# Prologue of a Fourier filter and MLP-mixer kernel: six inputs in flight, TensorE sums of first token weights and filter products, one table, a filter part on GpSimd's queue

## Chip, cores, metric

One core of one Trainium2 chip. The metric is device time in microseconds; each version was run several times on the chip that also ran the kernel before, and only runs of the same (fast) state are compared. "Faster" and "slower" need 2%. Single places in a trace are given as microseconds from the start of the span.

## The reference

```python
def _attn_ref(x, filt_r, filt_i):              # x (8, 3008, 256), filters (1505, 256)
    X = np.fft.rfft(x, axis=1)
    Y = X * (filt_r + 1j * filt_i)[None, :, :]
    return np.fft.irfft(Y, n=x.shape[1], axis=1).astype(np.float32)

def _moe_ref(x, w_tok1, w_tok2, w_ch1, w_ch2): # (3008,256) (256,3008) (256,1536) (1536,256)
    xt = x.transpose(0, 2, 1)
    h = np.maximum(xt @ w_tok1, 0.0) @ w_tok2
    u = x + h.transpose(0, 2, 1)
    return (u + np.maximum(u @ w_ch1, 0.0) @ w_ch2).astype(np.float32)
```

The weights come as float64; the kernel reads their words and rounds them to float32 itself ("conversion").

## The kernel before

The transform of length 3008 = 64 x 47 is done in two matmul stages. Here stage A is the length-64 transform of batch 0 (12 units, result z written to memory), stage B the 32 length-47 steps with the filter (`b_unit`: matmul and multiplication, `bi_unit`: inverse matmul), stage C the conversion of the second token weights and two channel-weight tiles; then the mixer starts, beside which the other batches are filtered. The parts that matter:

```python
    def rounded(st, n, parts, late=False):        # conversion of one weight tile
        ...
        nc.scalar.activation(out=top, in_=hi_f, func=AF.Copy, scale=2.0 ** -112)
        nc.vector.tensor_scalar(out=top_i, ...)            # four VectorE operations
        ...
        for src, dst in parts:                             # and the sum of the two halves
            nc.vector.tensor_tensor(out=dst, in0=src(top), in1=src(rest), op=ALU.add)

    def w1_fold(i):                               # first token weights times a DFT table
        ps = bank("po%d" % (i % 2))
        w = w1[:, 2 * i:2 * i + 2, :].rearrange("p a t -> p (a t)")
        nc.tensor.matmul(ps, wai_t, w, start=True, stop=True)
        nc.scalar.copy(out=w, in_=ps)

    def wc1_load(i, late=True):                   # channel weights: load, later convert, combine
        st = stage(512)                           # waits for a free stage buffer
        for g in range(CB):
            nc.gpsimd.dma_start(...)
        yield
        rounded(...)
        if c == DH - 1:
            combine(wc1[:, 2 * q:2 * q + 2])      # five GpSimd operations

    def weights():
        ...
        n = len(steps)                            # 12 + 16 + 2 tiles before the mixer
        steps += [f(i) for f, i in LAST]          # ten channel-weight tiles in the mixer
        ...
        load(AHEAD)                               # AHEAD = 6
        yield
        for i, s in enumerate(steps):
            next(s, None)                         # converts tile i
            load(not n - 2 <= i < n)              # loads one tile ahead, save in two places
            yield

    def b_unit(k):
        ps = bank(("b", "pg")[k % 2] if first else "b")...
        nc.tensor.matmul(ps, wbs[k // WC][:, k % WC, :], t2s[k // KC][:, k % KC], ...)
        ...
        nc.vector.tensor_tensor(out=p1, in0=ps, in1=fr, op=ALU.mult)
        nc.vector.scalar_tensor_tensor(out=p2[re], in0=ps[im], scalar=-1.0, in1=fi, ...)
        nc.vector.tensor_tensor(out=p2[im], in0=ps[re], in1=fi, op=ALU.mult)
        nc.vector.tensor_tensor(out=p1, in0=p1, in1=p2, op=ALU.add)
        prods[k] = p1
```

## Time and profile before

| | kernel before |
|---|---|
| time, median of 4 runs | 2663.66 us (2662.44 to 2665.65) |
| span and mean granted TensorE clock of the profiled run | 2662.7 us, 0.978 |
| first filter product (stage B begins) | 63.34 us |
| last filter product begins | 145.46 us |
| mixer's first matmul | 200.53 us |
| token sums of batch 1 | 552.23 us |
| last group of matmuls | 2643.01 us |

The last five are places of single instructions in the timeline. The granted clock is the share of full speed that the trace gives for TensorE. The stages by engine and the main waits are shown in the prediction.

### The profile page before, as it was taken

The numbers are of one execution on the slowest core, as the hardware profiler recorded it, in microseconds if no ns is written. First come the engines' busy times: TensorE is split into PE (matmuls) and PEld (weight loads), VectorE is DVE, ScalarE is ACT, GpSimd is POOL, SyncE is SP. The second block draws the span as 40 slices with busy tenths as digits, with TensorE's granted clock in tenths as the row PEclk, the third lists the DMA queues.
The fourth block names the chain that finished last, engine by engine and source line by source line (L and its number), as shares of the span: only waits on it lengthen the run. The fifth ranks groups of instructions, "written<-read, shape, count | busy, mean of one in ns | idle before, by whom it ended". The sixth has DMA issues, their size and how long they took to land.

```text
span 2662.7 us, 31542 instructions
## 1 busy us (share of the span) xinstructions
PE 2509.5 (94%) x10840; PEld 2000.5 (75%) x10840; DVE 1827.1 (69%) x3505; ACT 678.4 (25%) x1325; POOL 503.4 (19%) x926
## 2 busy tenths in 40 slices
PE   4667999999999999999999999999999999999997
PEld 1344766688787777788887777788888888888886
DVE  3886688846567788745658588755678586647675
ACT  2222322213222222212322122222222122212221
POOL 2324211111212111121211112121121121211221
PEclk8778999999999999999999999999999999999999
DMA  7664433222332222212233223211322111100000
GB/s 221 184 193 135 144 104 106 81 72 88 94 98 82 72 85 70 70 30 67 90 96 89 66 87 89 74 33 48 99 68 83 51 47 55 24 9 8 17 15 17
DMA packets 167158, 210.28 MB, mean 79 GB/s; under 512 B 35868, under 2 KB 115633, under 8 KB 166998
## 3 DMA queue, kind: packets, MB, share of 16 engines
q1 hardware_dynamic: 92937, 111.56, 13.9%
q0 software_dynamic: 30976, 44.53, 6.8%
q10 hardware_dynamic: 43085, 52.17, 6.0%
q8 instruction: 86, 1.41, 0.2%
q14 instruction: 74, 0.61, 0.1%
HBM read 133.15 MB, written 74.97 MB: 78 GB/s over the span
## 4 chain that ended last, share of the span: by engine, by line
PE 73%; DVE 18%; DMA 3%; issue 3%; ACT 2%; POOL 0%; SPq 0%; ACTq 0%; DVEq 0%; POOLq 0%
PE ps_po L526 25%; PE ps_pg L492 15%; PE ps_pg L508 11%; PE ps_acc L452 6%; PE ps_acc L435 5%; DVE t L470 3%; PE ps_acc L457 3%; DVE hh L470 3%; PE ps_b L382 3%; PE ps_b L349 3%; PE ps_acc L398 2%; DVE u L470 2%; DVE s L470 2%; DMA x<-in_x_dram 1%; DVE p L392 1%
## 5 line engine op out<-in xcount | busy, mean ns | idle before, releaser
L470 DVE TENSOR_TENSOR hh<-ps_pg,s 128x512 f32<-128x512 f32 (+3 forms) x864 | 482.7, 586 | 638.1 <-ACT s L495 637.5
L571 POOL DMA_DIRECT2D out_dram<-r x757 | 409.7, 550 | 1964.3 <-ACT hh L513 889.1
L513 ACT ACTIVATE hh<-hh 128x512 f32<-128x512 f32 (+1 forms) x576 | 347.9, 621 | 1110.6 <-DVE hh L470 1110.6
L526 PE MATMUL ps_po<-t,wc 128*128 128x256 f32 (+1 forms) x2304 | 536.1, 376 | 4.1 <-DVE t L470 3.0
L526 PEld LDWEIGHTS ps_po<-t,wc 128*128 128x128 f32 x2304 | 435.3, 190 | 127.8 <-issue 49.8
L492 PE MATMUL ps_pg<-v,wc 128*128 128x256 f32 (+1 forms) x1728 | 419.5, 380 | 2.5 <-POOL wc L275 2.4
L526 PE MATMUL ps_po<-hh,wc 128*128 128x256 f32 (+1 forms) x1728 | 413.5, 376 | 3.1 <-ACT hh L513 3.1
L492 PEld LDWEIGHTS ps_pg<-v,wc 128*128 128x128 f32 x1728 | 331.8, 193 | 43.3 <-POOL wc L275 2.8
L526 PEld LDWEIGHTS ps_po<-hh,wc 128*128 128x128 f32 x1728 | 328.5, 191 | 42.1 <-ACT hh L513 5.1
L508 PE MATMUL ps_pg<-u,wc 128*128 128x256 f32 (+1 forms) x1152 | 294.3, 378 | 9.1 <-DVE hh L470 9.0
L470 DVE TENSOR_TENSOR t<-t,hh 128x256 f32<-128x256 f32 (+1 forms) x576 | 243.5, 423 | 19.8
L508 PEld LDWEIGHTS ps_pg<-u,wc 128*128 128x128 f32 x1152 | 215.7, 190 | 48.6 <-DVE hh L470 23.6
L470 DVE TENSOR_TENSOR s<-ps_pg,hh 128x512 f32<-128x512 f32 (+1 forms) x288 | 196.1, 681 | 31.4 <-DVE hh L470 1.8
L452 PE MATMUL ps_acc<-w,h 128*128 128x512 f32 (+1 forms) x384 | 180.0, 591 | 15.8 <-ACT h L441 11.6
L470 DVE TENSOR_TENSOR t<-hh 128x512 f32<-128x512 f32 (+1 forms) x288 | 193.2, 671 | 0.6 <-ACT hh L513 0.6
L435 PE MATMUL ps_acc<-t,w 128*128 128x256 f32 x768 | 169.6, 383 | 6.2 <-DMA t<-g_tmp 5.0
L492 PE MATMUL ps_pg<-u,wc 128*128 128x256 f32 (+1 forms) x576 | 171.9, 381 | 0.4 <-DVE hh L470 0.4
L398 PE MATMUL ps_acc<-p,wi 128*96 128x512 f32 (+1 forms) x320 | 145.4, 537 | 26.5 <-DVE p L393 14.8
L508 PE MATMUL ps_pg<-v,wc 128*128 128x256 f32 (+1 forms) x576 | 168.9, 375 | 0.0
L435 PEld LDWEIGHTS ps_acc<-t,w 128*128 128x128 f32 x768 | 147.5, 193 | 27.7 <-issue 5.8
L382 PE MATMUL ps_b<-t,wb 96*128 96x512 f32 (+1 forms) x288 | 133.2, 545 | 21.9 <-DVE p L392 14.0
L495 ACT COPY s<-ps_pg 128x256 f32<-128x256 f32 (+1 forms) x288 | 105.8, 367 | 154.1 <-PE ps_pg L492 150.1
(67 smaller groups left out, 1949.5 us busy)
## 6 DMA issues: line engine op xcount, KB each, us to landing
z_tmp<-t ACTq DMA_DIRECT2D x96, 256.0 KB
t<-z_tmp SPq DMA_DIRECT2D x128, 192.0 KB
g_tmp<-t ACTq DMA_DIRECT2D x128, 192.0 KB
t<-g_tmp SPq DMA_DIRECT2D x48, 512.0 KB
x<-in_x_dram SPq DMA_DIRECT2D x184, 128.0 KB
out_dram<-r POOLq DMA_DIRECT2D x698, 32.0 KB, 1.8
wb<-wb_t SPq DMA_DIRECT2D x80, 96.0 KB
wi<-wi_t SPq DMA_DIRECT2D x80, 96.0 KB
```

The source lines that it names most:

```text
L349: nc.tensor.matmul(ps, wa, xs.pop((b, c)).rearrange("p a d -> p (a d)"), start=True, stop=True)
L382: nc.tensor.matmul(ps, wbs[k // WC][:, k % WC, :], t2s[k // KC][:, k % KC], start=True, stop=True)
L398: nc.tensor.matmul(ps[0:KR], wis[k // WC][:, k % WC, :], prods.pop(k), start=True, stop=True)
L435: nc.tensor.matmul(acc[:, t, :], w1[:, a, ts(t, P)], t4[b, a // TC4][:, a % TC4, :], start=(a == 0 and t == 0), stop=(a == A - 1 and t == ...
L452: nc.tensor.matmul(ps[:, 0:w], h1[:, t, ts(dh, P)], w2[:, t, ds(m * 512, w)], start=(t == 0), stop=False)
L470: nc.vector.tensor_tensor(out=out, in0=in0, in1=in1, op=op)
L492: nc.tensor.matmul(ps[:, 0:hw], wc1[:, jp, n, :], mov, start=True, stop=True)
L495: nc.scalar.copy(out=s[:, 0], in_=g[0][:, 0, 0:hw])
L508: nc.tensor.matmul(ps[:, 0:hw], wc1[:, jp, n, :], mov, start=True, stop=True)
L513: nc.scalar.activation(out=hs, in_=hs, func=AF.Relu)
L526: nc.tensor.matmul(po[i][:, j, 0:hw], wc2[:, jp, n, :], mov, start=(jp == 0 and first == 1), stop=(jp == JP - 1 and last == 1))
L571: q.dma_start(rows[g, e, :, ds(h * A + 4 * m, n)], blocks[ts(g, CW), h, e, 0:n])
```

## The change

The intent is to shorten the prologue: more inputs in flight in stage A; two VectorE sums (of the halves of a token-weight tile, of the two filter products) moved into TensorE's accumulation; one table load instead of two; the filter part that ScalarE's queue loaded moved to GpSimd's. The core of the diff:

```diff
-AHEAD = 6
+EARLY = 12
@@ on-chip sum of the halves, replacing rounded() + w1_fold() for first token weights
+    behind, banks = [], ["po%d" % i for i in range(4)]
+    def on_chip(stat, top, rest, n, parts):
+        banks.append(banks.pop(0))
+        def f(tag=banks[0]):
+            ps = bank(tag)[:, 0:n]
+            nc.tensor.matmul(ps, stat, top, start=True, stop=False)
+            nc.tensor.matmul(ps, stat, rest, start=False, stop=True)
+            for src, dst in parts:
+                nc.scalar.copy(out=dst, in_=src(ps))
+        behind.append(f)
@@ w1_load
+        q = nc.sync if i < EARLY else nc.gpsimd
-            nc.gpsimd.dma_start(st[...], rows[:, lo:lo + n, :])
+            q.dma_start(st[...], rows[:, lo:lo + n, :])
@@ weights
-        load(AHEAD)
-        yield
-        for i, s in enumerate(steps):
-            next(s, None)
-            load(not n - 2 <= i < n)
-            yield
+        ... # load() loads the next tile, rnd() converts the next one
+    def convert():
+        if len(behind) > 1:
+            behind.pop(0)()
+        round_tile()
+        load_tile()
@@ x_load, dft
+        where, tag = ((xp, "x"), (tp, "t"), (vp, "v"))[c % 3] if b == 0 else (xp, "x")
+        ahead = 3 * XB if first else XB
@@ load (tables, filter)
-                nc.sync.dma_start(wbs[g], wb_d[:, ts(g, WC), :])
-                nc.sync.dma_start(wis[g], wi_d[:, ts(g, WC), :])
-            filt_load(c, (nc.sync, nc.scalar, nc.gpsimd) if first else (nc.sync,) * 3)
+                nc.sync.dma_start(wbs[g], wbi_d[:, ts(g, WC), :])
+            filt_load(c, (nc.sync, nc.gpsimd, nc.gpsimd) if first else (nc.sync,) * 3)
@@ b_unit, bi_unit
-            nc.vector.tensor_tensor(out=p1, in0=p1, in1=p2, op=ALU.add)
+            if not first:
+                nc.vector.tensor_tensor(out=p1, in0=p1, in1=p2, op=ALU.add)
-            nc.tensor.matmul(ps[0:KR], wis[...], prods.pop(k), start=True, stop=True)
+            for i, p in enumerate(parts):
+                nc.tensor.matmul(ps[0:KR], wbs[...], p, start=(i == 0), stop=(i == len(parts) - 1))
@@ the driver of stages A and B: conversions in A at i = 5, 7, 9, 11, in B at every fourth step
```

## The prediction

> **What bounds the kernel now.** I first read the page's slices: TensorE is at 90% or more in all but the first few, so the batches after the first leave little to gain, and the change touches only what runs before them. I then cut the start of the trace into stages, whose borders I took from the timeline, and asked for each engine's busy time in each. The columns are stretch and length, busy us and instruction counts of TensorE, its weight loads, VectorE, ScalarE and GpSimd, then granted TensorE clock, DMA share, GB/s.
>
> ```profile
> 0.00:55.10 55.10, 26.71 (x31) 8.60 (x32) 17.38 (x28) 13.02 (x21) 15.66 (x34) 0.89 0.84 229
> 55.10:63.30 8.20, 4.40 (x8) 1.84 (x6) 2.93 (x5) 1.24 (x3) 3.47 (x7) 0.71 0.64 193
> 63.30:119.00 55.70, 33.89 (x80) 19.31 (x78) 46.59 (x102) 12.82 (x29) 16.56 (x29) 0.71 0.63 175
> 119.00:148.50 29.50, 21.48 (x60) 11.48 (x59) 23.53 (x57) 5.66 (x16) 8.11 (x15) 0.79 0.57 168
> 148.50:200.50 52.00, 32.47 (x123) 24.33 (x122) 47.81 (x106) 12.01 (x22) 15.89 (x29) 0.80 0.68 210
> ...
> 575.00:2645.00 2070.00, 2052.59 (x9229) 1689.05 (x9228) 1410.73 (x2718) 535.65 (x1052) 363.65 (x672) 1.00 0.21 62
> ```
>
> Stage A (0 to 55.1) is the length-64 transform of batch 0; the DMA engines are the busy ones. Then 8.2 us pass until VectorE gets the first product of stage B. B (63.3 to about 148) is the 32 length-47 steps with filter multiplication; VectorE is 82% busy. C (to 200.5) converts the second token weights and two channel-weight tiles; VectorE is 92% busy. From 575 on TensorE is 99% busy. So 200 us are the prologue, bounded by DMA first, then by VectorE.
>
> The waits before 60 us, and between 60 and 155 us, name the stalls (engine, line, releaser: total us, times, longest):
>
> ```profile
> PE ps_acc L349 <- DMA x<-in_x_dram: 25.7, 6, 7.4
> ```
> ```profile
> ACT t L403 <- PE ps_acc L398: 43.1, 21, 5.4
> PE ps_acc L398 <- DVE p L393: 14.8, 7, 4.1
> ACT both L219 <- DMA filt<-in_filt_r_dram: 8.9, 1, 8.9
> ```
>
> In A TensorE waits for inputs, of which two tiles are in flight. Between A and B ScalarE is held up 8.9 us by filter DMAs that it has to issue itself. In B TensorE waits for VectorE's sums. The groups by shape in the first 200 us give the costs (busy, mean ns of one):
>
> ```profile
> L393 DVE TENSOR_TENSOR p<-p,p 128x256 f32<-128x256 f32 x32 | 13.6, 426 | 1.1
> L227 DVE TENSOR_TENSOR w<-both 128x512 f32<-128x512 f32 x12 | 8.3, 691 | 0.4
> L247 PE MATMUL ps_po<-w,wai_t 128*128 128x512 f32 x24 | 18.9, 889 | 0.0
> L398 PE MATMUL ps_acc<-p,wi 128*96 128x256 f32 x64 | 27.9, 529 | 25.9 <-DVE p L393 14.8 <-issue 7.6 <-ACT t L403 3.2
> ```
>
> **What the Trainium skill says.** "TensorE: Matmul & The Clock Gate", Part 1: the array runs at half clock until it has been busy for about 3.4 us and falls back when idle. The trace agrees in kind: back-to-back f32 matmuls of 256 columns (two passes each) follow each other every 0.85 us in a slow stretch of B (139.6, 140.4) and every 0.43 us in a fast one (84.29, 84.73), and the mean clock in B is 0.71 to 0.79. "DMA: Bandwidth & Descriptors", "Issuing engines are not separate DMA queues": loads issued by any engine share the same 16 DMA engines, and a second issuer saves only issue time. In A the trace moves 229 GB/s at a share of 0.84 whatever queue carries it; dividing the two gives an estimate of 270 GB/s as ceiling for these packets. "SBUF — State Buffer", the note on the DVE blocking software DMA: GpSimd can't write descriptors while VectorE holds the shared port. The trace neither proves nor refutes it; a GpSimd DMA issue takes 0.53 to 0.57 us in B, now doubled in number.
>
> **The change part by part.** (a) Inputs. Six tiles instead of two are loaded ahead, and the token-weight loads, formerly six tiles at once on GpSimd's queue ahead of everything, now stand behind the first inputs on SyncE's. In program order ten of twelve weight tiles are still issued before the first load of B, on the same queue. By then must be moved: x 3.1 MB, ten tiles of 0.52 MB, z 3.1 MB, filter and tables 0.6 MB: 12.0 MB. At 245 to 260 GB/s (between measured rate and estimated ceiling) plus 2 us start that is 48 to 51 us; before, 12.6 MB had moved at 55. The A compute itself gets done sooner: by an estimate of 2.8 us a unit, near 36 us, since its inputs come first. But B's first load of z queues behind the weights. So the transform's own end doesn't set B's start; the bytes do.
>
> (b) Gap. The first filter tiles are loaded by GpSimd during A, where it has nothing else, and ScalarE issues none. The 8.9 us hold goes; the z write, its read-back and one matmul remain, about 3 us, partly inside (a). With (a), the first product comes at about 51 us instead of 63.3: 12 us.
>
> (c) B on VectorE. Four operations a step at a pitch of 0.44 us (141.53, 141.97, 142.41, 142.86 in the timeline) were 1.7 us with the last overlapped; three are 1.3. The 32 adds were 13.6 us, gone. A token-weight conversion was five operations: 0.43+0.69+0.43+0.69+0.69 = 2.93 us busy, about 3.0 with gaps; without the last it is 2.24, about 2.35 with gaps. B now holds nine conversions instead of six: 32 x 1.3 + 9 x 2.35 = 63 us, against 32 x 1.7 + 6 x 3.0 = 72 before (measured 85: 13 us of waits).
>
> (d) B on TensorE. Added: a second matmul for each of 32 steps and each of 12 weight tiles. At full clock a step is 3 x 0.43 = 1.3 us and a weight sum 2 x 0.85 = 1.7 us; over four steps 6.9 us against VectorE's 4 x 1.3 + 2.35 = 7.6. At half clock it would be 13.8 and TensorE the bound; but an engine that busy should mostly hold its clock. ScalarE's copy must free the one accumulating bank before the next sum begins, so about 1.5 us a step is the floor there.
>
> (e) B on DMA. The joint table tile is 128 x 448 x 4 = 229 KB against 98 + 98. Per two steps: z 197, g 197, table 229, filter 290, and 195 KB of weights on average: 1.1 MB. VectorE's pace of 1.9 us a step would need 290 GB/s; the fast part of B before (119 to 147, 1.72 us a step, 0.88 MB per two) ran at about 256 by the same sum. GpSimd issues 6.5 DMAs per two steps at 0.54: 3.5 us, 1.75 us a step. So VectorE, DMA and GpSimd are close together, and I choose 2.25 us a step with their interference: 72 us, against 84 before. That is 12 us.
>
> (f) C. One second-token-weight tile has moved into B. Such a tile takes 2.77 us here (conversions start at 152.12, 154.84 and 157.57). Saved: 3 us; the rest stays bounded by VectorE.
>
> Sum: 12 + 12 + 3 = 27 us. From there the mixer runs as before, with TensorE as bound, so the whole shift reaches the end; one table load instead of two saves issues there but no TensorE time. I add 1 us for it: 2664.5 - 28 = 2636.5 us.
>
> **The rivals.** First, B becomes bound by TensorE at half clock or by GpSimd's descriptors, so that the wait for VectorE only changes its name. For it: mean clock 0.71 in B, GpSimd's doubled issues, the single accumulation bank. Against: more continuous matmuls should raise the clock, and GpSimd has 8 us of lead. B would stay at 84 us, and the gain at about 15: 2650. Second, the DMA engines take the 12 MB faster once small software-issued traffic is gone, and B runs at VectorE's 63 us: 17 + 21 + 3, about 2623. Third, bandwidth in A was the only bound and B's first z loads queue even longer behind the weight tiles, whose buffers wait for conversions: the gain in (a) is 4 us, total 18: about 2646. Fourth, an earlier mixer start collides with channel-weight loads or the following batches' filter steps in 200 to 575 us, where TensorE isn't full (118 of 139.5 us, then 219 of 235): up to 10 us given back.
>
> **Range and chances.** The rivals span 2623 to 2650 singly; mixtures with D's uncertainty give 2619 to 2654 for eight in ten. Over 2% needs 53.3 us. VectorE's floor for B (63) with a start at 44 and C less 3 would be 19 + 21 + 3 = 43, so only an unseen saving in the first batch's mixer makes that: 0.04. Slower by 2% needs a new stall of 80 us: 0.01. Within 2%: 0.95.
>
> **What would show it right or wrong.** First product near 51 us (right from 47 to 55); the share of the DMA engines in A at 0.9 or more. Last product near 123, VectorE 85% busy between, granted clock above 0.85. No ScalarE wait on filter DMAs. The mixer's first matmul near 173 instead of 200.5, and token sums of batch 1 at about 524 instead of 552.4. If B's waits read TensorE waiting for ScalarE's copies or VectorE waiting for matmuls, the first rival holds; if for filter or z DMAs, my bandwidth term was too kind. If the mixer starts at 173 but the end moves less, the fourth. Wrong altogether would be a shift of the mixer's start under 10 us or over 45.

## The result, and the profile after

| | before | after |
|---|---|---|
| median (4 runs each) | 2663.66 us | 2669.56 us (2669.37 to 2670.48) |
| ratio to before, 95% interval | 1 | 1.0022 [1.0005, 1.0039] |
| span of the profiled run, clock | 2662.7 us, 0.978 | 2667.6 us, 0.982 |

A ratio is the mean time of one kernel's fast runs over that of the other's in the same rounds, so not quite the ratio of the medians. By the 2% rule the two are the same; the time rose by about 6 us where a fall of 28 was predicted, outside the predicted range.

First the ledger. Its pieces add up to the spans. The last column is a version with two repairs, found below; the "predicted" column is taken from the landmarks that the prediction names.

| piece of the span | before | after | predicted | both repairs |
|---|---|---|---|---|
| start to first filter product | 63.34 | 55.59 | 51 | 54.13 |
| first to last filter product (B) | 82.12 | 84.12 | 72 | 71.16 |
| last product to the mixer's first matmul (C) | 55.07 | 58.71 | 50 | 57.94 |
| from there to the token sums of batch 1 | 351.70 | 365.68 | 351 | 348.46 |
| from there to the last group of matmuls | 2090.78 | 2090.42 | as before | 2091.57 |
| last group of matmuls to the end | 19.69 | 13.08 | as before | 13.14 |
| span | 2662.70 | 2667.60 | | 2636.40 |

Stage A gained 7.75 us. B, which should have gained most, lost 2.0 (runs below with the same B took 80.3 in place of 82.1 and 85.5 in place of 84.1, so the size is rough); C lost 3.6; the first batch's mixer lost 14.0; and the end of the program gained 6.6 that nobody had asked for.

The stages of the kernel after (columns as in the prediction's first fence):

```profile
0.00:38.00 38.00, 22.43 (x29) 7.11 (x30) 9.45 (x15) 10.37 (x17) 11.05 (x24) 0.81 0.79 235
38.00:55.60 17.60, 4.11 (x7) 1.77 (x6) 2.25 (x5) 1.43 (x3) 0.00 (x0) 0.60 0.98 257
55.60:139.70 84.10, 64.53 (x215) 36.94 (x215) 56.49 (x125) 20.27 (x46) 46.19 (x85) 0.95 0.66 188
139.70:198.40 58.70, 38.42 (x136) 27.18 (x136) 49.19 (x109) 12.73 (x24) 14.97 (x28) 0.77 0.60 189
564.00:2655.00 2091.00, 2073.86 (x9328) 1704.19 (x9327) 1410.12 (x2718) 537.98 (x1056) 372.50 (x688) 1.00 0.22 62
```

In B VectorE is busy only 67% (56.49 of 84.10), down from 80% and more: its work fell as intended, and the stage didn't follow. TensorE is 77% busy at a clock of 0.95. So no engine is full, and neither are the DMA engines (0.66): something makes them wait for each other.

Between A and B, the waits of the kernel after (38 to 60 us):

```profile
PE ps_b L413 <- DMA t<-z_tmp: 13.5, 1, 13.5
DVE p L426 <- PE ps_b L413: 11.2, 1, 11.2
```

And SyncE's own queue from 33 to 56 us (start, us, engine, line):

```profile
34.56 12.98 SPq L266 DMA_DIRECT2D st<-in_moe_w_tok_dram  x13
...
49.81 0.33 SPq L409 DMA_DIRECT2D t<-z_tmp  x1
```

The matmuls of A end at 38 us; then TensorE waits for z, whose loads are issued at 49.81 behind 13 of token weights, with the DMA engines 98% busy. 38.0 x 235 + 17.6 x 257 is 13.45 MB by the first product.

The waits of B (60 to 145 us):

```profile
ACT t L442 <- PE ps_acc L437: 52.8, 25, 4.3
DVE both L215 <- ACT both L214: 19.2, 7, 2.9
...
PE ps_acc L437 <- DVE p L426: 15.9, 8, 2.3
```

The second line has grown: VectorE waits 2.7 us in each of seven conversions for ScalarE's activation. Before, the same wait was 7.4 us in six (60 to 155 us):

```profile
DVE both L220 <- ACT both L219: 7.4, 6, 2.2
```

The last line of the kernel after says that TensorE then waits for VectorE. One such place in the timeline of the kernel after:

```profile
100.54 1.02 PE L249 MATMUL ps_po<-both,wai_t 128*128 128x512 f32 x2
...
101.40 1.02 PE L250 MATMUL ps_po<-both,wai_t 128*128 128x512 f32 x2
...
102.46 0.59 ACT L252 COPY w<-ps_po 128x512 f32<-128x512 f32 x1 [1.35 <-PE ps_po L250]
...
102.94 0.67 ACT L214 ACTIVATE both<-st 128x512 f32<-128x512 f32 x1
...
103.64 0.43 DVE L215 TENSOR_SCALAR both<-both 128x512 uint32<-128x512 uint32 x1 [2.71 <-ACT both L214]
```

Read upwards: VectorE's first operation of a conversion (L215) waited for ScalarE's activation (L214), which needs nothing but a loaded tile, but stands in ScalarE's queue behind the copy (L252) of an earlier tile's sum, which waits for TensorE's two matmuls (L249, L250), which stand behind those of the filter. In `convert()` the sum that stood behind is emitted ahead of the next tile's conversion; the kernel before did it the other way round (`next(convert)`, then `w1_fold`). "Perfetto Trace Analysis" in the Trainium skill, section "Per-engine timelines", says that ScalarE, VectorE and GpSimd are strict FIFO; the trace agrees, with the activation starting 0.48 us after the copy at 102.46. A group of four steps takes 10.35 us (L215 at 103.64 and 113.99).

The mixer's start. TensorE's waits from 195 to 260 us, before:

```profile
PE ps_pg L492 <- POOL wc L275: 2.4, 1, 2.4
```

and after:

```profile
PE ps_pg L531 <- POOL wc L299: 9.9, 1, 9.9
PE ps_po L565 <- POOL wc L300: 6.1, 1, 6.1
```

Both are waits for GpSimd's combination of channel weights. GpSimd's timeline before:

```profile
190.07 0.75 POOL L292 DMA_DIRECT2D st<-in_moe_w_ch_dram  x1 [0.21 <-issue]
199.86 0.85 POOL L272 TENSOR_SCALAR wc<-wc 128x256 f32<-128x256 f32 x1 [9.04 <-DVE wc L227]
```

and after:

```profile
187.72 0.75 POOL L316 DMA_DIRECT2D st<-in_moe_w_ch_dram  x1
203.63 1.94 POOL L306 DMA_DIRECT2D st<-in_moe_w_ch_dram  x4 [15.16 <-issue]
205.72 0.86 POOL L296 TENSOR_SCALAR wc<-wc 128x256 f32<-128x256 f32 x1
```

Before, the combination waits 9.04 us for VectorE, that is for its data. After, four DMA issues stand ahead of it, and ahead of those lie 15.16 us of idle time. The old generator left out the load ahead in two places, `load(not n - 2 <= i < n)`: the last two conversions before the mixer. The new `convert()` always loads. The stage buffers of the late tiles are four, so the load issued there waits for a buffer that only a conversion inside the mixer frees, and the combination waits behind it in GpSimd's queue.

C. The last four u matmuls (two products of 512 columns, two passes each), before and after:

```profile
197.82 1.98 PE L452 MATMUL ps_acc<-w,h 128*128 128x512 f32 x4 [0.73 <-ACT u L459]
```
```profile
193.93 3.75 PE L491 MATMUL ps_acc<-w,h 128*128 128x512 f32 x4 [0.73 <-ACT u L498]
```

The same work takes nearly double; from 175 to 200 us the granted clock is 0.55 after and 0.73 before. The first matmuls that use the last tile of second token weights began at 193.70 in the kernel before, 6.83 us ahead of the mixer's first matmul; after, at 189.42, 9.00 us ahead. That is 2.2 of the 3.6 us lost in C. It can't be booked to the change: these four matmuls take 3.75 to 3.78 us in nine of the fourteen traces, e_before_nohold (the old kernel with one condition removed) among them, and 1.98 or 1.99 us in the other five, e_swap among them. Another 1.4 us are lost at C's start, where VectorE waits 3.98 us for ScalarE's activation, against 2.16 before.

The end. GpSimd's drain, its DRAIN instructions at the end of the program (count, then shortest/median/longest ns), before and after:

```profile
L732 POOLq DRAIN  x3: 46/97/9702, 2652.2 to 2662.4; - x3
```
```profile
L774 POOLq DRAIN  x3: 46/98/3098, 2663.7 to 2667.3; - x3
```

In both kernels the first drain starts 9.2 us after the last group of matmuls; the longest of the three takes 9.7 us before and 3.1 after. The difference of 6.6 us is this one instruction.

### The profile page after: what moved, and what is told of

Same layout as the page of the kernel before. It is cut to its first block, busy times and chain, and to the rows that moved or that the text cites. A ratio compares the mean times of both kernels' runs of the same rounds, so it can differ in the third digit from the quotient of the medians.

```text
span 2667.6 us, 31529 instructions
## 1 busy us (share of the span) xinstructions
PE 2520.6 (94%) x10928; PEld 2003.2 (75%) x10928; DVE 1802.7 (68%) x3461; ACT 678.9 (25%) x1325; POOL 516.0 (19%) x951
## 4 chain that ended last, share of the span: by engine, by line
PE 72%; DVE 14%; issue 2%; ACT 1%; DVEq 0%; SPq 0%; DMA 0%; ACTq 0%; POOL 0%; POOLq 0%
PE ps_po L565 25%; PE ps_pg L531 15%; PE ps_pg L547 11%; PE ps_acc L491 6%; PE ps_acc L474 5%; PE ps_acc L496 3%; DVE t L509 3%; DVE hh L509 3%; PE ps_b L413 3%; PE ps_b L381 2%; PE ps_acc L437 2%; DVE u L509 2%; DVE s L509 2%; DVE p L428 1%; DVE p L427 1%
## 5 line engine op out<-in xcount | busy, mean ns | idle before, releaser
L547 PE MATMUL ps_pg<-u,wc 128*128 128x256 f32 (+1 forms) x1152 | 295.4, 379 | 11.2 <-DVE hh L509 11.1
L437 PE MATMUL ps_acc<-p,wb 128*96 128x256 f32 (+1 forms) x384 | 157.1, 501 | 18.5 <-DVE p L426 15.9
L474 PEld LDWEIGHTS ps_acc<-t,w 128*128 128x128 f32 x768 | 146.8, 192 | 26.3 <-ACT both L214 4.1
```

The costliest lines, as they stand in the source:

```text
L437: nc.tensor.matmul(ps[0:KR], wbs[k // WC][:, k % WC, P:], p, start=(i == 0), stop=(i == len(parts) - 1))
L474: nc.tensor.matmul(acc[:, t, :], w1[:, a, ts(t, P)], t4[b, a // TC4][:, a % TC4, :], start=(a == 0 and t == 0), stop=(a == A - 1 and t == ...
L547: nc.tensor.matmul(ps[:, 0:hw], wc1[:, jp, n, :], mov, start=True, stop=True)
```

## The experiments

Twelve runs, all correct, with 3 rounds each (4 runs of the kernel, 7 of the one before). Medians come from four jobs, each on a chip of its own, so the ratio to before is the number to compare across jobs.

| run | median us | ratio to before [95%] | us against e_both, by the ratios |
|---|---|---|---|
| e_hold | 2656.09 | 0.9971 [0.9956, 0.9986] | +15.5 |
| e_swap | 2656.89 | 0.9972 [0.9957, 0.9987] | +15.7 |
| e_both | 2640.12 | 0.9913 [0.9896, 0.9929] | 0 |
| e_before_nohold | 2678.01 | 1.0054 [1.0039, 1.0069] | +37.6 |
| e_defer | 2639.44 | 0.9907 [0.9892, 0.9922] | -1.6 |
| e_two_inputs | 2639.00 | 0.9903 [0.9886, 0.9919] | -2.7 |
| e_filt_dve | 2648.49 | 0.9939 [0.9924, 0.9954] | +6.9 |
| e_queues | 2652.42 | 0.9955 [0.9941, 0.9970] | +11.2 |
| e_late | 2641.29 | 0.9915 [0.9900, 0.9930] | +0.5 |
| e_w1_dve | 2651.86 | 0.9962 [0.9945, 0.9978] | +13.1 |
| e_early0 | 2636.17 | 0.9901 [0.9886, 0.9915] | -3.2 |
| e_w1_twice | 2646.30 | 0.9933 [0.9917, 0.9950] | +5.3 |

The last column is the difference of the two ratios times 2664 us. The kernel after stands at +29.0 in it.

### The two repairs

**e_hold**: the kernel after, without the load ahead in the last two conversions before the mixer.

```diff
-    def convert():
+    def convert(ahead=True):
         ...
-        load_tile()
+        if ahead:
+            load_tile()
         ...
         for _ in range(DH):
-            convert()
+            convert(False)
```

> The changed kernel, but no channel-weight tile is loaded ahead at the last two conversions before the mixer, as the kernel before had it. Theory H (GpSimd's in-order queue: a load that waits for a stage buffer stands ahead of the first weight combination, which the mixer's second matmul needs): the two waits of TensorE for GpSimd's combinations in the first batch (9.9 and 6.1 us in the changed kernel) shrink to about 2.5 and 0, the mixer's second group of matmuls starts near 201 instead of 208.9, the token sums of batch 1 near 550 instead of 564.1, and the time falls by 12 to 14 us, give or take 7 for the end of the program, whose GpSimd drain was 9.7 us in the kernel before and 3.1 in the changed one. Rival (collision of the earlier mixer with the following batches' transfers): loads ahead fewer by two change nothing or make it worse: token sums of batch 1 at 564 or later.

Measured: 13.5 us less than the kernel after (here and in the next three runs by the medians; the ratios agree within 1 us). GpSimd's timeline again:

```profile
189.00 0.75 POOL L316 DMA_DIRECT2D st<-in_moe_w_ch_dram  x1
196.89 0.85 POOL L296 TENSOR_SCALAR wc<-wc 128x256 f32<-128x256 f32 x1 [7.13 <-DVE wc L239]
```

The combination waits for its data again, 8.8 us earlier than in the kernel after. The token sums of batch 1 come at 552.43, as before the change (552.23).

**e_before_nohold**: the reverse, in the old kernel.

```diff
-            load(not n - 2 <= i < n)
+            load(True)
```

> The kernel before with the one condition removed that kept it from loading ahead at the last two conversions before the mixer. Theory H: the two waits for GpSimd's combinations appear in it too (about 10 and 6 us against 2.4 and 0), token sums of batch 1 go from 552.2 to about 565, and the time rises by 12 to 14 us, less up to 7 where the end of the program drains faster. Rival (the waits belong to the earlier start or to the new queues of the change): no change within 2 us.

Measured: 14 us more than the kernel before, with the same two waits:

```profile
PE ps_pg L492 <- POOL wc L275: 9.9, 1, 9.9
PE ps_po L526 <- POOL wc L276: 5.3, 1, 5.3
```

So this one condition, and nothing else of the change, is the loss at the mixer's start.

**e_swap**: the kernel after, with the next tile's conversion emitted ahead of the sum that stands behind.

```diff
     def convert():
+        round_tile()
         if len(behind) > 1:
             behind.pop(0)()
-        round_tile()
         load_tile()
```

> The changed kernel, but each conversion step starts the new tile's rounding before the earlier tile's TensorE sum and its copy. Theory S (ScalarE's queue: the copy of the TensorE sum stands ahead of the next tile's first rounding step, and the sum stands behind the filter matmuls, so VectorE waits 2.7 us in each of nine conversions): the VectorE waits for that step (25.8 us in B) fall under 8, a group of four steps takes about 7.8 us instead of 10.36, B's last product comes near 121 instead of 141, and the time falls by about 18 us as far as the two GpSimd waits do not grow. Rivals: if GpSimd's doubled filter loads or the DMA engines bound B, the group of four stays at 9 us or more and VectorE's waits turn up at filter or z loads; if TensorE's second matmuls bound it, they turn up at the matmuls.

Measured: 12.7 us less than the kernel after. First to last product takes 75.0 us instead of 84.1. The waits for the activation didn't fall below 8 us in all as I had expected, but, in B alone, from 21.8 (55 to 140 us) to 9.0 (55 to 130 us); a group of four steps takes 9.0 us, not 7.8. The edit was the cure for the loss, and a rest of the chain stays. One thing goes with the new order: since a tile now joins `behind` before the test of its length, each sum comes one conversion sooner than in the kernel after. On every other engine the order within a conversion is unchanged, and the trace shows the wait on ScalarE; but no run separates the order from the sooner sum.

**e_both**: both edits.

> Both edits. If H and S hold and are independent: token sums of batch 1 near 530, the time 30 to 35 us under the changed kernel, 2635 to 2640, which is what the prediction said for the change itself. If they overlap, the mixer's start shifts but a wait for channel weights, whose loads then come sooner after the second token weights, takes over: 2645 to 2655.

Measured: 2640.12 us, 29.4 less than the kernel after, 0.9913 of the kernel before. In its timeline the activation now comes ahead of the copy:

```profile
92.53 0.67 ACT L214 ACTIVATE both<-st 128x512 f32<-128x512 f32 x1 [0.43 <-DVE p L429]
...
93.23 0.43 DVE L215 TENSOR_SCALAR both<-both 128x512 uint32<-128x512 uint32 x1 [1.05 <-ACT both L214]
...
93.45 0.59 ACT L252 COPY w<-ps_po 128x512 f32<-128x512 f32 x1 [0.25 <-PE ps_po L250]
```

VectorE waits 1.05 us here instead of 2.71. The two repairs add up to a little less than both together (13.5 + 12.7 = 26.2). How far one trace can be trusted: e_swap and e_both have the same program up to the end of B, and yet B took 75.0 us in the one and 71.2 in the other, so differences of up to 4 us in B between two traces mean little. All further runs start from this version, so that each part of the change can be undone by itself.

### The parts of the change, one at a time

**e_two_inputs** undoes the six inputs in flight.

```diff
-        ahead = 3 * XB if first else XB
+        ahead = XB
```

> Base: the kernel with both repairs, 2640.1 us. Undoes the six inputs in flight (two, as before), alone. The input stage then waits for its inputs one after the other as in the kernel before, but what bounds the start of the filter stage is the sum of the bytes ahead of it, and the order of the queue (SyncE) stays. If bytes alone bound it, the first product stays within 2 us of 54.1 and the total within 2 us of 2640. If six inputs carry the gain that the change was meant to have, the first product comes 4 to 9 us later (58 to 63 us, as in the kernel before) and the total at 2644 to 2649. My own guess is the latter, nearer its low end, since input loads waiting for a buffer block SyncE's queue, with the weight tiles behind them.

Measured: ratio 0.9903 against 0.9913, no difference; the first product comes at 54.96 instead of 54.13. I had leaned to a loss of 4 us, wrongly. The inputs in flight bring nothing that shows in the time: the bytes ahead of B set its start. The profiled execution, though, is the slowest of the four (2644.76 us, the others 2637.03 to 2639.27), and in it B took 76.5 us; why, no run shows.

**e_filt_dve** lets VectorE sum the filter products again.

```diff
-            if first:
+            if False:                      # p2 in its own tile, one product in prods
                 p1, p2 = p1[:, 0:1], p1[:, 1:2]
-            if not first:
-                nc.vector.tensor_tensor(out=p1, in0=p1, in1=p2, op=ALU.add)
+            nc.vector.tensor_tensor(out=p1, in0=p1, in1=p2, op=ALU.add)
```

> Base: the kernel with both repairs, 2640.1 us, in which VectorE is busy 57.9 of 75.1 us of the filter stage. Undoes the TensorE sum of the filter product alone: a fourth VectorE operation of 0.41 us in each of 32 steps and one matmul less. VectorE then has 57.9 + 32 x 0.41 = 71 us of work in that stage. If the stage follows VectorE's work when it is near full (term (e) of my prediction, 12 us for this part with the first-weight sums), the stage grows by 6 to 13 us and the total goes to 2646 to 2653. If the stage is held by the chain from TensorE over ScalarE (the order of its queue), 0 to 3 us.

Measured: 6.9 us more by the ratios (8.4 by the medians), within what was expected. First to last product takes 79.1 us instead of 71.2. So this part of the change brings what was intended; but not shown is that VectorE's work alone is the reason. This edit also takes a matmul off TensorE in every step, and from 56 to 120 us the granted clock is 0.84 instead of 0.99, and an inverse matmul takes 482 ns instead of 392. The runs e_w1_dve and e_w1_twice below separate the two for the other sum; for this one, no run does.

**e_queues** gives the second filter part back to ScalarE's queue.

```diff
-            filt_load(c, (nc.sync, nc.gpsimd, nc.gpsimd) if first else (nc.sync,) * 3)
+            filt_load(c, (nc.sync, nc.scalar, nc.gpsimd) if first else (nc.sync,) * 3)
```

> Base: the kernel with both repairs, 2640.1 us. Undoes the move of a doubled filter part from ScalarE's queue to GpSimd's alone: ScalarE issues it again, about 0.5 us for each of three or four issues in 16 pairs of steps, ahead of its copies. I expect ScalarE's copies of the inverse step to come up to 1.5 us later in every second step, of which little is on the path: total 2639 to 2645. A second question: the long drain of GpSimd at the program's end, 9.7 us in the kernel before and 3.1 us in all the changed ones. If it follows the filter part's queue it goes back to 9.7 us here (total +6.6 us, 2646); if it follows the first token weights' queue it stays at 3.1.

Measured: 11.2 us more, above the 5 us I expected at most. Two things are in it. B is 7.6 us longer (78.8): ScalarE's copies of the inverse step now wait behind the filter loads in its queue, as I read the waits of 55 to 146 us:

```profile
ACT t L443 <- DMA filt<-in_filt_r_dram: 17.3, 8, 4.1
```

And the drain is long again, by 4.3 us, though not as long as before:

```profile
L775 POOLq DRAIN  x3: 46/98/7413, 2641.2 to 2649.1; - x3
```

**e_early0** gives the first token weights back to GpSimd's queue.

```diff
-EARLY = 12
+EARLY = 0
```

> Base: the kernel with both repairs, 2640.1 us. Undoes the queue of the first token weights alone: their tiles go to GpSimd's queue, as before, not SyncE's. SyncE's queue then holds no tile ahead of the loads of z; if that order is what delays the first product, it comes at 46 to 50 us as in the run e_defer; if bytes alone do, at 53 to 55 us. GpSimd, which also issues the two filter parts at the filter stage, then waits in order for the weights' stage buffers, so filter loads come later: I expect the filter stage 3 to 10 us longer and a total of 2640 to 2650. The second question is GpSimd's drain at the end of the program (9.7 us before, 3.1 us in most changed kernels, 7.4 us in the run e_queues, which gives GpSimd one filter part less): if the number of transfers on GpSimd's queue sets it in no simple way, it will be some other value; if having the weights there makes it long, 9 to 10 us.

Measured: 2636.17 us, not slower as I expected. The first product comes at 51.79 us and B is no longer (70.8 us). That first product lies between the two times that I had named (46 to 50 us for the order of the queue, 53 to 55 for the bytes): with no weight tile ahead of z on SyncE's queue it came only 2.3 us sooner, with the DMA engines 98% busy from 38 us on, so most of the wait is bytes. The interval of its ratio overlaps much of that of e_both, so what can be said is that moving these loads to SyncE, part of the change, brought nothing. The drain was 3.66 us: it isn't the token weights' queue that makes it long.

**e_w1_dve** lets VectorE sum the halves of the first token weights again; TensorE makes one matmul for each tile.

```diff
-        on_chip(wai_t, *halves(st, 512, spare_pair()), 512, [(lambda v: v, w1[...])])
+        w = w1[:, 2 * i:2 * i + 2, :].rearrange("p a t -> p (a t)")
+        rounded(st, 512, [(lambda v: v, w)], False)
+        on_chip(wai_t, w, None, 512, [(lambda v: v, w)])
@@ on_chip
-            nc.tensor.matmul(ps, stat, top, start=True, stop=False)
-            nc.tensor.matmul(ps, stat, rest, start=False, stop=True)
+            nc.tensor.matmul(ps, stat, top, start=True, stop=True)
```

> Base: the kernel with both repairs, 2640.1 us. Undoes the TensorE sums of the first token weights alone: VectorE adds the two rounded halves again (one operation of 0.4 us for each of 12 tiles, eight in the filter stage) and TensorE makes one matmul of 0.86 us instead of two. If VectorE is what bounds the filter stage (my prediction's terms (c) and (e)), the stage grows by 8 x 0.4 = 3.3 us or more: 2643 to 2646. If TensorE and the chain behind it hold the stage (65.2 of 75.1 us busy, ScalarE waiting 43.8 us for the inverse matmuls), it shrinks by up to 8 x 0.86 = 6.9 us: 2634 to 2638. I lean to the middle: 2638 to 2643, so this part of the change brings little.

Measured: 13.1 us more by the ratios, above all I expected. VectorE's additional work is 8 x 0.69 = 5.5 us in B (the 0.4 in my expectation was wrong, the row in the prediction has 0.69); B grew by 13.4 (to 84.6). The groups of inverse matmuls from 56 to 120 us, with both repairs, then here:

```profile
L438 PE MATMUL ps_acc<-p,wb 128*96 128x256 f32 x112 | 31.0, 392 | 4.1 <-DVE p L427 3.2 <-DVE p L429 0.6
```
```profile
L438 PE MATMUL ps_acc<-p,wb 128*96 128x256 f32 x96 | 34.7, 493 | 10.4 <-DVE p L427 9.9 <-DVE p L429 0.5
```

The same matmul takes 493 ns instead of 392, and the granted clock in this stretch is 0.80 instead of 0.99. With less TensorE work, TensorE's matmuls were slower. To see whether that is a cause:

**e_w1_twice**: e_w1_dve with the one matmul simply done twice into the same bank.

```diff
-            nc.tensor.matmul(ps, stat, top, start=True, stop=True)
+            for _ in range(2):
+                nc.tensor.matmul(ps, stat, top, start=True, stop=True)
```

> Base: the run e_w1_dve (VectorE adds the halves of the first token weights, one TensorE matmul each), 2651.9 us, against 2640.1 us with both repairs. Undoing that part cost 11.7 us, far more than the 8 x 0.7 us of VectorE work it adds in the filter stage. In its trace the granted clock of 56 to 120 us is 0.80 against 0.99, and an inverse matmul of 128x256 takes 493 ns in the mean against 392. Here the one fold matmul is simply done twice into the same bank, with the same result: the same VectorE work as in e_w1_dve, and the TensorE work of the kernel with both repairs. If the extra loss is the TensorE clock, which falls when TensorE has too little to do, the clock comes back to 0.93 or more, the inverse matmul to about 400 ns, and the total to 2640 to 2646. If it is VectorE's extra work or the order of the work alone, the useless matmul brings nothing or costs up to 5 us more: 2651 to 2657, with the clock perhaps higher.

Measured: by the ratios 7.7 us less than without the useless matmul, by the medians 5.6 (the intervals of the two ratios overlap a little, between 0.9945 and 0.9950; the trace agrees, with 78.6 us for B instead of 84.6, and a clock of 0.95):

```profile
L439 PE MATMUL ps_acc<-p,wb 128*96 128x256 f32 x100 | 29.3, 411 | 6.5 <-DVE p L428 5.6 <-DVE p L430 0.6
```

So about half of what e_w1_dve lost comes back with TensorE's work alone, and the clock with it; the 5.3 us that remain against e_both would fit VectorE's 5.5 us of work, but the intervals of these two runs overlap too.

### The bytes ahead of B

**e_defer** keeps four of the ten token-weight tiles back, behind B's first loads.

```diff
                 if i in (5, 7, 9, 11):
-                    convert()
+                    convert(False)
                     rounds += 1
             elif (i - NXC) % 4 == 2:
                 convert()
                 rounds += 1
+            elif i - NXC in (0, 4, 8, 12):
+                load_tile()
```

> Base: the kernel with both repairs (no load ahead in the two conversions before the mixer; conversion before the TensorE sum that stands behind), 2640.1 us. There the first filter product comes at 54.1 us after a 14.3 us wait of VectorE, with the DMA engines 98% busy at 246 GB/s and 13.4 MB moved by then; ten tiles of first token weights (0.52 MB each) go to SyncE's queue ahead of the first loads of the length-47 step. Here the last four of the ten are put behind those loads, into the filter stage. If the first product waits for bytes that stand ahead of it in the queue (the step of my prediction that 'Rival 3' doubted), it comes 2.1 MB / 246 GB/s = 8.5 us earlier, at 45 to 48 us. What of it is kept: the two stages together move 29.5 MB, which at 247 GB/s is 119.6 us against 129.2 us now, so the filter stage may turn into one that waits for its own loads; I expect the last product 4 to 8 us earlier and the total 2632 to 2636. If instead the wait is the latency of the round trip through memory (writes of z, then the reads), the first product stays at 52 to 54 us and the total at 2640.

Measured: the first product comes at 46.48 us, 7.65 earlier, as the queue's bytes demand (expected 45 to 48), and the time stays (0.9907 against 0.9913): the seventeenth product comes at 91.50, against 90.86 with both repairs. In the stages of this run one sees a likely reason:

```profile
60.00:75.00 15.00, 10.05 (x32) 6.20 (x33) 8.29 (x20) 2.74 (x6) 7.70 (x15) 0.89 0.96 219
75.00:90.00 15.00, 10.38 (x37) 6.48 (x36) 9.10 (x21) 3.09 (x7) 10.25 (x19) 0.92 1.03 247
```

The DMA engines are full (shares of 0.96 and 1.03, at 219 and 247 GB/s) where the four tiles now come.

**e_late** loads them in the second half of B instead.

```diff
-            elif i - NXC in (0, 4, 8, 12):
+            elif i - NXC in (16, 20, 24, 28):
```

> Base: the kernel with both repairs, 2640.1 us. Keeping four tiles of first token weights back (the run e_defer) brought the first filter product from 54.1 to 46.5 us, but the seventeenth came at 91.5 instead of 90.9 us, with the DMA engines 96 to 103% busy from 60 to 90 us: the four tiles were loaded then, so that the gain was given back. Here they are loaded in the second half of the filter stage instead (one at steps 16, 20, 24 and 28), where the DMA engines are 63 to 84% busy. If bytes set the pace up to step 16, the seventeenth product comes 5 to 8 us earlier (83 to 86 us), later steps run at their own 2.25 us each, and the last product and the total come 4 to 8 us earlier: 2632 to 2636. If the pace from 54 us on is set by TensorE, VectorE and ScalarE (TensorE is busy 65.2 of 75.1 us), the total stays at 2638 to 2641.

Measured: 0.9915, again no gain. The first sixteen steps keep their lead longer (the thirteenth product at 74.94 instead of 81.87), then the seventeenth comes at 87.83 and the last at 125.75, against 125.29. From 90 to 105 us the DMA engines move 281 GB/s at a share of 1.00. A gain in A can be moved through B but not kept with these loads; I didn't find out whether another placing would keep it.

## Why the prediction was wrong

**Inputs and gap, (a) and (b): 12 us predicted, 7.75 measured.** The mechanism held: the bytes ahead of z in the queue set B's start (e_defer), not the inputs in flight (e_two_inputs), and ScalarE's hold of 8.9 us is gone. The mis-sized term is the bytes: 13.45 MB had moved by then, not 12.0; the mean rate, 242 GB/s, was just under the assumed 245 to 260. The loads that the trace shows as issued by then hold 1.8 MB of filters and tables, where the sum had 0.6, and 0.6 MB of z read back, which it left out. And that hold was not what set B's start before: it ended at 65.70 us, after the first product at 63.34, which itself had waited 4.00 us for a filter load.

**VectorE's and TensorE's work in B, (c) and (d): right in the main.** VectorE was busy 56.5 us in B (63 predicted, gaps included, with nine conversions where eight fall into it; eight make 60), and the clock rose to 0.95 as expected. TensorE was busy 64.5 us, where eight groups of 6.9 make 55.

**B's length, (e): failed.** "VectorE, DMA and GpSimd are close together, and I choose 2.25 us a step" summed each engine's work and left out the order in which one queue carries two chains. In the kernel after, a conversion waits for the sum of an earlier tile through ScalarE's queue; a step took 84.12 / 31 = 2.71 us. With the order mended, it took 71.16 / 31 = 2.30. One figure under the choice was misread, too: "1.72 us a step" and "about 256" GB/s for 119 to 147 us of the kernel before. In that stretch 14 products start, 2.0 us a step, and its own first table has 168 GB/s for nearly the same stretch. (The 84 us there also count to the end of the last step; from first to last product it was 82.12.) The first rival had B at its old length, but by a half-rate clock or GpSimd's issues, and neither was so: the clock was 0.95 and GpSimd busy 55%. The sign it named, VectorE waiting for others, was seen, but the reason was an order in the diff that I could have read in `convert()`.

**C, (f): failed.** The ninth conversion of B falls after the last product, so 18 tiles are left for C as before, and nothing is saved. Instead 3.6 us were lost: 1.4 at C's start, for ScalarE's activation, and 2.2 at its end, with the slow u matmuls that come and go between traces.

**"From there the mixer runs as before": failed, and this is the largest step.** 14.0 us were lost there. My fourth rival expected a collision with channel-weight loads, of up to 10 us, from an earlier start of the mixer. There was a collision with such a load, but not because of an earlier start: the dropped condition put it ahead of the combination (e_hold takes it away, e_before_nohold brings it into the old kernel). The line stood in the diff, and I took it for a rewriting of the generator.

**Not foreseen: 6.6 us gained at the end**, in GpSimd's drain. Without it the kernel after would have been slower by more. It also means that e_both's 2640 us is close to my 2636.5 partly by luck: up to the last group of matmuls it gains 19.75 us, and the drain gives the rest of its 26.3 us of span.

**What stays open.** Why the drain is long in some versions: 9.7 us (before, and e_before_nohold), 7.4 (e_queues), 3.1 to 3.7 (the others). Giving the second filter part back to ScalarE's queue made it 7.4 instead of 3.1, so that queue has a part in it; what makes up the rest, and by what mechanism, no run shows. The part "one table instead of two" was not tried alone.

## What to carry to other kernels

When a diff restructures the loop that emits instructions, read the new order for each in-order queue, and ask of every condition that vanishes what it held back: here one dropped "don't load now" cost 14 us and two lines in the wrong order 13, which hid a gain of 24 (6.6 of it the drain). Sums of work by engine tell only what a stage could take; what it takes is set by which instruction stands ahead of which in the queue of an engine that isn't full. And work taken off TensorE in a stage where it already pauses can cost more than it saves, since its clock may fall.

## What the Trainium skill lacked or had wrong

- "TensorE: Matmul & The Clock Gate", Part 1, is right in kind. What these runs add is a trade that the effect spoils: with one matmul of 128x512 fewer for each weight tile and one VectorE sum more, the clock from 56 to 120 us was 0.80 instead of 0.99, and doing that matmul a second time for nothing brought it to 0.95 and saved 5.6 us (medians; 7.7 by the ratios).
- "DMA: Bandwidth & Descriptors", "Issuing engines are not separate DMA queues", says that a second issuer saves only the time to issue. Here moving one filter part from GpSimd's to ScalarE's queue lengthened stage B by 7.6 us; as I read the waits, the issuer's other work stands in order behind the loads (17.3 us of ScalarE's waits, in 8 copies). The page doesn't mention that.
- No page that I read says what sets the length of GpSimd's drain at the end of a program: 3.1 to 9.7 us here, all of it on the end of the span.
